# Writing out the order of four engines by hand in a fused RWKV-5 and multiplicative-FFN kernel

## The chip, the cores and the metric

One core of one Trainium2 chip. The metric is the device time of one execution in microseconds (us). Engines are called by their names in the profile: PE is the TensorE (matrix products), ACT the ScalarE, DVE the VectorE, SP the SyncE, which in these profiles only issues transfers. PSUM is the memory that TensorE's products go to here; another engine reads a bank of it out before the next product goes into it (in the changed kernel TensorE waits 9.5 us in all, three times, for a copy that does this).

## The reference, cut to what matters

```python
# attention: B, H, S, D = 4, 8, 768, 48; float32
for t in range(S):
    y[:, :, t] = r_t @ (state + (u * k_t) outer v_t)
    state = w * state + k_t outer v_t
# feed-forward on 3072 tokens of width 384; its weights come as float64
x = y.transpose(0, 2, 1, 3).reshape(3072, 384)
out = ((x @ w1) * (x @ w2)) @ w3 @ w_out      # w1, w2: 384 x 1024; w3: 1024 x 1024; w_out: 1024 x 384
```

## The kernel before

The sequence is cut into six chunks of 128 steps; a chunk of one batch row is a "unit" (24 in all). A unit costs TensorE about 2.6 us; after four units a chunk has 512 tokens, and the feed-forward takes them in eight "pairs" (x·w1 and x·w2 for 128 columns, 5.15 us a pair). w3 and w_out are multiplied with each other once ("folding"), so that the output of a chunk is then a product with one 1024 x 384 matrix, done as seven products of halves with sums of halves (Strassen-Winograd). The weights arrive as float64 and are turned into float32 by integer work shared between ScalarE and VectorE:

```python
def convert(piece, raw):                                   # 8 pieces of w1/w2, 8 of w_out, 16 of w3
    ...
    nc.scalar.activation(out=power, in_=hi.bitcast(F32), func=ABS)
    nc.vector.tensor_scalar_max(power, power, 2.0 ** -15)
    nc.vector.tensor_scalar(tb, hi, 0x80000000, None, ALU.bitwise_and)
    nc.vector.scalar_tensor_tensor(hb, pb, 3, tb, ALU.logical_shift_left, ALU.bitwise_xor)
    nc.scalar.activation(out=t, in_=lo, func=IDENTITY, bias=two, scale=2.0 ** -51)
    nc.vector.tensor_add(hb, hb, tb)
```

A load lands in one of three raw buffers. The diagonal of a unit (the u term) is three operations on VectorE and eight on ScalarE. A visit of a unit begins with the diagonal of the next one, then does half of the feed-forward steps planned beside it, then the unit's output and the next unit's products, then the other half:

```python
def diagonal(n):
    nc.vector.tensor_mul(ruk, kr[:, 0], kr[:, 1])
    nc.vector.tensor_mul(ruk, ruk, ub)
    nc.vector.tensor_reduce(dg, ruk, AX.X, ALU.add)
    for p in range(NP):
        for i in range(2):
            nc.scalar.activation(out=AT[n][:, i, p, :], in_=same, func=COPY, scale=dg[:, h:h + 1])
...
for b in range(B):                       # one visit
    scale(n + 1); diagonal(n + 1)        # or turn_rows(n + 1): ScalarE's copy of kT
    scale(n + 2); turn_blocks(n + 2)     # VectorE
    for step in plan[2 * b]: step()
    output(n)
    pairs(n + 1)
    for step in plan[2 * b + 1]: step()
```

The products of the feed-forward and of the output take turns in two PSUM banks (pool psF). What frees the first output product is a copy on ScalarE; the others are freed by additions on VectorE:

```python
def o(c, m):
    def product(a, b):
        ps = psF.tile([P, DH], F32, tag="f", ...)            # two banks
        ...
    nc.scalar.copy(out=m1, in_=product("a11", "b11"))
    nc.vector.tensor_add(top[:, :DH], product("a12", "b21"), m1)
    nc.vector.tensor_add(u2, product("s2", "t2"), m1)
    ...
```

In this kernel the order of the source is only a wish: a scheduler decides which instruction comes next on each engine.

Of the kernel before, what the change touches and what calls it, by code (L numbers as in the profile page):

```python
# [8 lines left out]
F32 = mybir.dt.float32  # L9
# [7 lines left out]
IDENTITY = mybir.ActivationFunctionType.Identity  # L17
PSUM = bass.MemoryType.PSUM


@with_exitstack
def kernel(
# [86 lines left out]
    two = const.tile([P, 1], F32)  # L109
    nc.vector.memset(two, 2.0)  # L110
# [18 lines left out]
    def load(n, which="krv"):  # L129
# [4 lines left out]
        for nm, src, dst in (("k", k, krin[n % NIN][:, 0]), ("r", r, krin[n % NIN][:, 1]), ("v", v, vnat[n % NV][:, :, :D])):  # L134
            if nm in which:
# [7 lines left out]
    ab_pieces = [(dst[:, z], src.rearrange("(q p) n -> p q n", p=P)[:, :, z * STRIP:(z + 1) * STRIP])  # L143
                 for z in range(DF // STRIP) for dst, src in ((w1, moe_w1), (w2, moe_w2))]
    sent = [0]

    def fetch(piece):

        dst, src = piece
        if src.dtype != U64:  # L150
            nc.sync.dma_start(out=dst, in_=src)
            return None
        _, m, n = src.shape
        raw = raws[sent[0] % NRAW][:, :m * n].rearrange("p (m n) -> p m n", m=m)
        sent[0] += 1
        nc.sync.dma_start(out=raw, in_=src)
        return raw
# [7 lines left out]
    landed = {0: fetch(ab_pieces[0])}  # L165
# [4 lines left out]
    landed[1] = fetch(ab_pieces[1])  # L170
# [47 lines left out]
    def body(arm, fast):  # L218
# [35 lines left out]
        def convert(piece, raw):  # L254
            dst, src = piece
            if src.dtype != U64:
                return
            _, m, n = src.shape
            lo, hi = (raw.bitcast(U32).rearrange("p m (n z) -> p m n z", z=2)[:, :, :, z] for z in range(2))
            t, power = (once.tile([P, RAW], F32, tag="cv", bufs=3 if fast else 2, name=nm)[:, :m * n].rearrange("p (m n) -> p m n", m=m)  # L260
                        for nm in ("t", "power"))
            tb, hb, pb = t.bitcast(U32), dst.bitcast(U32), power.bitcast(U32)



            nc.scalar.activation(out=power, in_=hi.bitcast(F32), func=ABS)  # L266
            nc.vector.tensor_scalar_max(power, power, 2.0 ** -15)  # L267
            nc.vector.tensor_scalar(tb, hi, 0x80000000, None, ALU.bitwise_and)
            nc.vector.scalar_tensor_tensor(hb, pb, 3, tb, ALU.logical_shift_left, ALU.bitwise_xor)  # L269

            nc.scalar.activation(out=t, in_=lo, func=IDENTITY, bias=two, scale=2.0 ** -51)  # L271
            nc.vector.tensor_add(hb, hb, tb)

        def weight(piece):
            convert(piece, fetch(piece))


        wo, w3n = {}, {}

        def out_weight(c):  # L280
            wo[c] = once.tile([P, DM], F32, tag="wo", bufs=KF, name=f"wo{c}")
            weight((wo[c][:, None, :], moe_w_out[c * P:(c + 1) * P, None, :]))

        def w3_weight(j, z):
            if z == 0:
                w3n[j] = once.tile([P, DF], F32, tag="w3", bufs=3, name=f"w3n{j}")
            js = slice(z * PIECE, (z + 1) * PIECE)
            weight((w3n[j][:, None, js], moe_w3[j * P:(j + 1) * P, None, js]))

        def fold(j):  # L290
            w3T = once.tile([P, KF, P], F32, tag="w3", bufs=3, name=f"w3T{j}")
            for i in range(2):
                ps = psF.tile([P, KF // 2, P], F32, tag="f", name=f"ps_w3T{j}_{i}")
                for q in range(KF // 2):
                    kc = i * (KF // 2) + q
                    nc.tensor.transpose(ps[:, q, :], w3n[j][:, kc * P:(kc + 1) * P], ident)
                nc.scalar.copy(out=w3T[:, i * (KF // 2):(i + 1) * (KF // 2), :], in_=ps)  # L297
            ps = psF.tile([P, DM], F32, tag="f", name=f"ps_w34_{j}")
            for kc in range(KF):
                nc.tensor.matmul(ps, lhsT=w3T[:, kc, :], rhs=wo[kc], start=(kc == 0), stop=(kc == KF - 1))  # L300
            nc.scalar.copy(out=w34[:, j, :], in_=ps)
# [12 lines left out]
        def diagonal(n):  # L314

            kr = krin[n % NIN]
            ruk = work.tile([C, H, D], F32, tag="ruk", bufs=1, name=f"ruk{n}")
            dg = work.tile([C, H], F32, tag="dg", bufs=2, name=f"dg{n}")
            nc.vector.tensor_mul(ruk, kr[:, 0], kr[:, 1])
            nc.vector.tensor_mul(ruk, ruk, ub)  # L320
            nc.vector.tensor_reduce(dg, ruk, AX.X, ALU.add)
            AT[n] = work.tile([C, 2, NP, T], F32, tag="AT", bufs=2, name=f"AT{n}")
            for p in range(NP):
                for i in range(2):
                    h = 2 * p + i
                    nc.scalar.activation(out=AT[n][:, i, p, :], in_=same, func=COPY, scale=dg[:, h:h + 1])  # L326
# [3 lines left out]
        def turned(n):  # L330
            kT[n] = work.tile([P, NP, C], F32, tag="kT", bufs=1, name=f"kT{n}")
            if fast:
                rT[n] = tts[n % 2][:, :, NP:].rearrange("x z p t -> x p z t")
            else:
                rT[n] = tts[n % 2].rearrange("x z e t -> x (z e t)").rearrange("x (e t) -> x e t", t=C)[:, NP:]

        def turn(n):
            turned(n)
            for g, dst, nm in ((0, kT, "kT"), (1, rT, "rT")):
                ps = psT.tile([P, NP, C], F32, tag="t", name=f"ps_{nm}{n}")  # L340
                for p in range(NP):
                    nc.tensor.transpose(ps[:, p, :], krs[n % NS][:, g, 2 * p:2 * p + 2, :].rearrange("t h d -> t (h d)"),
                                        ident)
                nc.scalar.copy(out=dst[n], in_=ps.rearrange("x p (z t) -> x p z t", t=Q) if fast and g else ps)
# [3 lines left out]
        scratch = {}  # L348

        def turn_blocks(n):  # L350
            tr = work.tile([P, 3, 2 * NP, Q], F32, tag="tr", bufs=1, name=f"tr{n}")
            nc.vector.transpose(out=tr.rearrange("x m e t -> x e m t"), in_=krs[n % NS][:, :, :, :D])  # L352
            scratch[n] = dram.tile([C // Q, Q, 3, Q * 2 * NP], F32, tag="scratch", bufs=2, name=f"scratch{n}")
            nc.sync.dma_start(out=scratch[n].rearrange("z f m e -> (z f) (m e)"), in_=tr.rearrange("x m e t -> x (m e t)"))
# [14 lines left out]

        def pairs(n):  # L370

            c, b = units[n]
            kk = krs[n % NS][:, 0]
            if fast:
                au = psA.tile([C, 2, 512], F32, tag="a", name=f"ps_a{n}")
                ps = au[:, :, :NP * T].rearrange("s i (p t) -> s i p t", p=NP)
            else:
                for l in range(LEVELS):
                    level(n, l)
                kk = work.tile([C, H, PAD], F32, tag="rl", bufs=1, name=f"kk{n}")  # L380
                nc.gpsimd.tensor_mul(kk, krs[n % NS][:, 0], pn[:, 0])
                au = psA.tile([C, 2, 512], F32, tag="a", name=f"ps_u{n}")

            up = au[:, :, NP * T:NP * (T + D)].rearrange("x a (p e) -> x a p e", p=NP)
            last = c == NCH - 1
            for p in range(NP):
                for i in range(2):
                    for a in range(1 if last else 2):
                        nc.tensor.matmul(up[rows(i), a, p, :], lhsT=kk[rows(a), 2 * p + i, :],  # L389
                                         rhs=vnat[n % NV][rows(a), 2 * p + i, 0:D], start=True, stop=True)  # L390
            if fast:
                for p in range(NP):
                    for a in range(2):
                        for i in range(2):
                            nc.tensor.matmul(ps[rows(a), i, p, :], lhsT=kT[n][rows(i), p, rows(a)],  # L395
                                             rhs=rT[n][rows(i), p, 2 * a:2 * a + 2], start=True, stop=True)
            by = wc.to_broadcast([P, NP, D])
            if c:
                spread(0, n)
            for a in range(1 if last else 2):  # L400
                if not c and not a:
                    if fast:
                        nc.vector.tensor_mul(st[b], up[:, a], by)
                    else:
                        nc.vector.tensor_copy(out=st[b], in_=up[:, a])
                elif fast:

                    nc.vector.tensor_add(st[b], up[:, a], st[b])
                    nc.vector.tensor_mul(st[b], st[b], by)
                else:  # L410
                    nc.vector.tensor_mul(st[b], st[b], by)
                    nc.vector.tensor_add(st[b], up[:, a], st[b])
                if not a:
                    spread(1, n)
            if fast:
# [262 lines left out]
```

## Time and profile before

| | before |
|---|---|
| median time, 4 executions | 526.04 us (525.05 to 526.63) |
| span of the profiled execution | 522.9 us |
| end of the first chunk's last pair ("the start") | 100.3 us |
| first output product begins | 232.8 us |
| from there to TensorE's last product ("the late part") | 285.9 us |

The last three rows are read from TensorE's records: the end of the 120th product of the pairs, the begin of the first 192-column product, the end of the last. 2860 TensorE products precede the first output product and 2332 are from it on. Each mark is read from one profiled execution.

### The profile page before, as it was taken

What the parts mean: (1) busy time and instruction counts of PE and PEld (TensorE: products, weight loads), DVE (VectorE), ACT (ScalarE), POOL (GpSimd) and SP (SyncE); (2) the same over time, 40 slices, a digit from 0 to 9 for tenths busy, and PEclk for the clock granted to TensorE, in tenths of its full rate; (3) what the DMA queues carried; (4) which work ended last, traced back from release to release, by engine and by line L of the source; (5) the groups of instructions that cost most, each with busy time, mean ns of one, the idle gap of its engine ahead of it and who ended that gap; (6) DMA issues with size and microseconds to landing.
All of it is one profiled execution on the core that took longest, in us unless ns stands there. A gap on an engine that the chain in (4) does not pass through costs nothing.

```text
span 522.9 us, 12272 instructions
## 1 busy us (share of the span) xinstructions
PE 495.6 (95%) x5192; PEld 324.3 (62%) x5192; DVE 281.8 (54%) x616; ACT 195.7 (37%) x487; POOL 6.0 (1%) x23
## 2 busy tenths in 40 slices
PE   2697999999999999999999999999999999999996
PEld 2586455455555656649646965498555777954486
DVE  5899897579766567492733374234432216211441
ACT  3897485566655667330223124222243110001000
POOL 4000000000000000000000000000000000000000
PEclk9887999999999999999999999999999999999999
DMA  8998565758684464230131324011120000000001
GB/s 207 230 239 236 151 149 143 197 176 207 156 253 120 164 185 117 48 91 31 57 81 45 93 77 107 32 58 50 42 77 21 1 32 31 32 30 1 0 7 60
DMA packets 96866, 52.73 MB, mean 101 GB/s; under 512 B 77729, under 2 KB 88226, under 8 KB 96802
## 3 DMA queue, kind: packets, MB, share of 16 engines
q1 hardware_dynamic: 96802, 51.86, 36.5%
q8 instruction: 43, 0.70, 0.6%
q14 instruction: 21, 0.17, 0.1%
HBM read 39.65 MB, written 12.19 MB: 99 GB/s over the span
## 4 chain that ended last, share of the span: by engine, by line
PE 85%; DVE 6%; ACT 4%; SPq 2%; issue 2%; DMA 1%; DVEq 0%; ACTq 0%
PE ps_b L505 22%; PE ps_a L500 22%; PE ps_w L300 8%; PE ps_y L483 4%; PE ps_y L473 3%; PE ps_s3t L539 3%; PE ps_s4b L539 3%; PE ps_s1t L539 3%; PE ps_a22t L539 3%; PE ps_a12b L539 3%; PE ps_s2t L539 3%; PE ps_a11b L539 3%; PE ps_a L395 2%; PE ps_a L389 1%; ACT AT L326 1%
## 5 line engine op out<-in xcount | busy, mean ns | idle before, releaser
L500 PE MATMUL ps_a<-xT,w 128*128 128x512 f32 (+1 forms) x300 | 134.8, 586 | 0.0
L505 PE MATMUL ps_b<-xT,w 128*128 128x512 f32 (+1 forms) x300 | 133.2, 578 | 0.2 <-DVE abt L506 0.2
L505 PEld LDWEIGHTS ps_b<-xT,w 128*128 128x128 f32 x300 | 56.2, 190 | 66.1 <-issue 59.6
L506 DVE TENSOR_TENSOR abt<-ps_b,a 128x512 f32<-128x512 f32 (+1 forms) x50 | 33.4, 669 | 116.6 <-PE ps_b L505 116.6
L500 PEld LDWEIGHTS ps_a<-xT,w 128*128 128x128 f32 x300 | 56.1, 192 | 58.4 <-issue 53.0
L502 ACT COPY a<-ps_a 128x512 f32<-128x512 f32 (+1 forms) x50 | 28.4, 569 | 148.4 <-PE ps_a L500 138.0
L326 ACT ACTIVATE AT<-same,dg 128x64 f32<-128x64 f32 x192 | 48.7, 336 | 0.3
L420 ACT COPY wide<-st 64x192 f32<-64x192 f32 x88 | 30.7, 348 | 43.2 <-PE ps_y L473 27.1
L300 PE MATMUL ps_w<-wo,w3T 128*128 128x384 f32 x128 | 43.1, 490 | 2.3 <-ACT w3T L297 2.3
L300 PEld LDWEIGHTS ps_w<-wo,w3T 128*128 128x128 f32 x128 | 23.7, 190 | 17.8 <-ACT w3T L297 2.8
L473 PEld LDWEIGHTS ps_y<-tt,wide 128*32 128x32 f32 x1056 | 18.4, 112 | 23.7 <-issue 15.9
L310 DVE TENSOR_TENSOR krs<-krin,pn_in 128x768 f32<-128x768 f32 x24 | 22.9, 956 | 18.1 <-PE ps_a L389 9.6
L473 PE MATMUL ps_y<-tt,wide 128*32 128x64 f32 x1056 | 25.3, 226 | 6.3 <-ACT wide L420 3.6
L271 ACT ACTIVATE t<-raw,two 128x512 f32<-128x512 uint32 (+2 forms) x32 | 25.4, 801 | 10.9 <-DVE wo L269 5.7
L266 ACT ACTIVATE power<-raw 128x512 f32<-128x512 f32 (+2 forms) x32 | 22.4, 706 | 10.6 <-DMA raw<-in_moe_w_dram 9.7
L483 PE MATMUL ps_y<-AT,vnat 64*64 64x64 f32 x1152 | 24.2, 232 | 1.6 <-DVE AT L416 1.6
L483 PEld LDWEIGHTS ps_y<-AT,vnat 64*64 64x64 f32 x1152 | 20.7, 144 | 6.4 <-DVE AT L416 2.0
L545 ACT COPY m<-ps_a11b 128x192 f32<-128x192 f32 x12 | 3.8, 319 | 53.5 <-PE ps_a11b L539 53.5
L267 DVE TENSOR_SCALAR power<-power 128x512 f32<-128x512 f32 (+2 forms) x32 | 14.0, 439 | 10.8 <-ACT power L266 10.6
L488 ACT COPY xT<-ps_y 128x384 f32<-128x384 f32 x24 | 11.4, 475 | 21.4 <-PE ps_y L483 15.8
L395 PE MATMUL ps_a<-tt,kT 64*64 64x64 f32 x768 | 18.3, 230 | 0.7 <-issue 0.7
L352 DVE STREAM_TRANSPOSE tr<-krs 128x768 f32<-128x768 f32 x19 | 18.6, 977 | 0.5
(92 smaller groups left out, 582.0 us busy)
## 6 DMA issues: line engine op xcount, KB each, us to landing
raw<-in_moe_w_dram SPq DMA_DIRECT2D x16, 512.0 KB, 4.7
scratch<-tr SPq DMA_DIRECT2D x19, 384.0 KB, 3.1
raw<-in_moe_w_dram SPq DMA_DIRECT2D x8, 768.0 KB, 5.5
tt<-scratch SPq DMA_DIRECT2D x38, 128.0 KB, 2.7
krin<-in_k_dram SPq DMA_DIRECT2D x24, 192.0 KB, 4.0
krin<-in_r_dram SPq DMA_DIRECT2D x24, 192.0 KB, 4.3
vnat<-in_v_dram SPq DMA_DIRECT2D x24, 192.0 KB, 3.6
out_dram<-osb SPq DMA_DIRECT2D x24, 192.0 KB, 1.9
```

What stands on the lines that cost most here:

```text
L271: nc.scalar.activation(out=t, in_=lo, func=IDENTITY, bias=two, scale=2.0 ** -51)
L300: nc.tensor.matmul(ps, lhsT=w3T[:, kc, :], rhs=wo[kc], start=(kc == 0), stop=(kc == KF - 1))
L326: nc.scalar.activation(out=AT[n][:, i, p, :], in_=same, func=COPY, scale=dg[:, h:h + 1])
L395: nc.tensor.matmul(ps[rows(a), i, p, :], lhsT=kT[n][rows(i), p, rows(a)], rhs=rT[n][rows(i), p, 2 * a:2 * a + 2], start=True, stop=True)
L420: nc.scalar.copy(out=wide[a][n % 2][rows(i), :, i * D:(i + 1) * D], in_=st[units[n][1]][rows(i)])
L473: nc.tensor.matmul(to(a, q, g), lhsT=wide[a][n % 2][:, p, j * Q:(j + 1) * Q], rhs=rw[:, p, 2 * a:2 * a + 2] if fast else rw[:, p, rows(a)] ...
L483: nc.tensor.matmul(ps[rows(g), a, q, :], lhsT=vv[rows(a), x:x + PAD], rhs=AT[n][rows(a), h % 2, h // 2, :], start=(a not in held and (a, g ...
L500: nc.tensor.matmul(pa[:, :n], lhsT=w1[:, z, q, js], rhs=xT[c][:, q, ts], start=(q == 0), stop=(q == KM - 1))
L502: nc.scalar.copy(out=a[:, :n], in_=pa[:, :n])
L505: nc.tensor.matmul(pb[:, :n], lhsT=w2[:, z, q, js], rhs=xT[c][:, q, ts], start=(q == 0), stop=(q == KM - 1))
L506: nc.vector.tensor_mul(abt[c, j][:, ts], pb[:, :n], a[:, :n])
L539: nc.tensor.matmul(ps, lhsT=made[c, j][a][:, m * C:(m + 1) * C], rhs=made[b][:, j, :], start=(j == 0), stop=(j == KH - 1))
```

## The change

The intent: in the start TensorE has holes since VectorE is full and works on the wrong things first, so the order of four engines is written down by hand, and for certainty the rest of the first path is placed in written order too. Conversions lose one operation; w3 is transposed one block ahead of its use; its loads are issued by ScalarE; four of the first diagonals are placed by VectorE.

```diff
+START = """
+d.0 N.0 e.0 M.0 k.0 f.0 T.0 H.0 g.0 U.0 R.0 d.1 i.0 k.1 p.0 e.1 r.0 kr.2 ...
+ ... (one word per step, 271 words, to the last pair of the first chunk)
+U.8 l.8 u.0.6.2 S.7 i.8 p.8 V.7 j.8 A.8 z.9 Y.7 a.0.7.2 m.8 b.0.7.2 c.0.7.2 u.0.7.2
+"""
 ... conversion
-            nc.scalar.activation(out=power, in_=hi.bitcast(F32), func=ABS)
-            nc.vector.tensor_scalar_max(power, power, 2.0 ** -15)
+            nc.scalar.activation(out=dst, in_=words(i)[1].bitcast(F32), func=ABS, scale=2.0 ** -112)
-            nc.scalar.activation(out=t, in_=lo, func=IDENTITY, bias=two, scale=2.0 ** -51)
+            nc.scalar.activation(out=part["t", i], in_=words(i)[0], func=COPY, scale=2.0 ** -29)
 ... w_out and w3: five operations of a piece spread over three steps, loads from ScalarE
+        def convert_on(i):
+            for step, x in ((total, i - 2), (magnitude, i), (high, i - 1), (sign, i), (low, i - 1)):
+                if NAB <= x < len(pieces):
+                    step(x)
+            if NAB < i:
+                fetch(i - 1 + NRAW, nc.scalar)
 ... the plan behind the start
+        def late(rest, folds, cut):
+            visits(2, merge(rest, folds[:cut]))
+            visits(3, ... + [sums_of_weights] + SUMS(0)[:2] + AB(2, range(1, 2)) + SUMS(0)[2:] + ... + O(0) + ...)
+            visits(4, O(1) + merge(SUMS(2), AB(3, range(3))) + O(2) + AB(3, range(3, KF)))
+            visits(5, merge(SUMS(3), AB(4, range(3))) + O(3) + AB(4, range(3, KF)))
+            for step in merge(SUMS(4), AB(5, range(3))) + O(4)[:1] + AB(5, range(3, KF)) + SUMS(5) + O(4)[1:] + O(5):
+                step()
+            with tc.manual_schedule(engines={PE, ACT, DVE, SP}):
+                for name, *at in (word.split(".") for word in START.split()):
+                    names[name](*map(int, at))
+                for i in range(NAB, NAB + NRAW):
+                    fetch(i, nc.scalar)
+                late(AB(1, ...), FOLD(convert_on, 2), 25)
```

(The letter of a word is a step, the number its unit or piece: d, e and f are VectorE's three operations of a diagonal, M, N, H, L and Q the five operations of a conversion, a and b the products of a pair, c and u ScalarE's copy and VectorE's multiplication behind them. Cut: the helpers that split a unit into steps, the second set of buffers for the sums, the general path for other values of w, which this input does not take.)

## The prediction

> **What bounds the kernel now.** I read the page's busy shares first, then the slices, the waits of the TensorE, narrow windows, the timeline. Shares and slices (a digit is tenths of a slice of 13.1 us, a fortieth of 522.9):
>
> ```profile
> PE 495.6 (95%) x5192; PEld 324.3 (62%) x5192; DVE 281.8 (54%) x616; ACT 195.7 (37%) x487; POOL 6.0 (1%) x23
> ...
> PE   2697999999999999999999999999999999999996
> ...
> DVE  5899897579766567492733374234432216211441
> ACT  3897485566655667330223124222243110001000
> ...
> PEclk9887999999999999999999999999999999999999
> ```
>
> TensorE is the bound; the only slices under 9 are the first four and the last. VectorE (DVE) is fullest exactly there, and the granted clock is lower there. So there is something to win only in the first 55 us or so, and a little later. How much, the waits of the TensorE tell:
>
> ```profile
> PE ps_p L208 <- DVE both L205: 7.6, 1, 7.6
> PE ps_y L473 <- ACT wide L420: 3.6, 3, 2.1
> PE ps_y L473 <- issue: 2.4, 2, 2.0
> PE ps_w L300 <- ACT w3T L297: 2.3, 3, 1.0
> PE ps_kT L342 <- DVE krs L310: 1.8, 1, 1.8
> PE ps_y L483 <- DVE AT L416: 1.6, 2, 1.3
> PE ps_kT L342 <- ACT kT L344: 1.3, 1, 1.3
> ```
>
> Without the first row (the preamble, which stays) and the small rows this is 13.0 us, of which L300 (2.3 us) is the folding of w3 into w_out. Windows (us, busy per engine with instructions, clock, DMA share, GB/s):
>
> ```profile
> 20.00:40.00 20.00, 17.66 (x446) 14.88 (x438) 19.54 (x39) 19.10 (x53) 0.00 (x0) 0.85 0.94 246
> 40.00:60.00 20.00, 16.48 (x192) 11.79 (x192) 19.16 (x36) 12.73 (x28) 0.00 (x0) 0.83 0.79 218
> ...
> 280.00:300.00 20.00, 19.65 (x280) 18.02 (x279) 8.82 (x21) 5.75 (x18) 0.00 (x0) 1.00 0.33 90
> 300.00:320.00 20.00, 20.00 (x191) 11.83 (x190) 13.32 (x33) 5.57 (x15) 0.00 (x0) 1.00 0.35 91
> ```
>
> From 20 to 60 us VectorE has no idle time; what matters is which work it does first. From 300 to 500 us TensorE never stops: there the scheduler's order leaves nothing to win, and a new order can only lose.
>
> [...] TensorE is busy only 1.49 of the 5 us from 40 us on, and from 45 to 50 us the clock is 0.50; six 256-column matmuls take 2.77 us there against 1.46 elsewhere. Window by window of 5 us from 15 to 50 us, busy time times the missing clock share is 0.2 + 1.0 + 1.3 + 0.3 + 2.5, about 5 us lost. [...] Here an issue takes some 0.4 us and landing 4.4 us (below)[...]. [...] the trace has 691 ns for the 128x512 multiplication. I take 0.69 us for the new diagonal.
>
> **The change part by part.** Durations, from the groups by line and the issues:
>
> ```profile
> L326 ACT ACTIVATE AT<-same,dg 128x64 f32<-128x64 f32 x192 | 48.7, 336 | 0.3
> ...
> L267 DVE TENSOR_SCALAR power<-power 128x512 f32<-128x512 f32 (+2 forms) x32 | 14.0, 439 | 10.8 <-ACT power L266 10.6
> ...
> raw<-in_moe_w_out_dram SPq DMA_DIRECT2D x8, 384.0 KB, 4.4
> ```
>
> *Shorter conversion.* Removes the 32 maximum operations, 14.0 us of VectorE, 8 of them (556 ns each, 4.4 us) in the first 60 us. *Diagonals on VectorE for units 1, 3, 5, 7.* ScalarE loses 4 x 8 activations (eight take 2.0 us in the timeline, so 8 us), VectorE gains 4 x 0.69 = 2.8 us. Neither engine is the bound beyond the start, so both matter only there.
>
> *Written order of the start (to the end of the first chunk's eight w1/w2 pairs).* In the timeline of before this work ends at 100.2 us, having begun at 11.4. TensorE's own work in it: 8 pairs x 5.15 + 9 units x 2.5 + 5 turned units x 1.2 = 70 us. Of the 89 us, 9.3 are idle and about 5 lost to the clock. Going down the written list with the durations of before, VectorE's list is 69 us long, so it is over at 80 us at the earliest and still sets the pace to about 65 us; after that TensorE does, and I get 87 us with no hand-over costs. I take 89: **gain 11 us** (7 to 13).
>
> *Folding, in strict order.* Now every instruction of the first path, not only the start, stays in written order, and the w_out/w3 conversions begin only after the start is over (the scheduler had put the first two w_out loads at 55 and 60 us). 13 conversion steps precede the first turn of w3, which stands after four pairs and two units: 4 x 5.15 + 2 x 2.6 = 26 us of TensorE work. Three raw buffers allow a load for every step only when the step two before has given its buffer up, so two steps take a landing (4.4) plus a step on ScalarE (0.55 + 0.65 + 0.4 for issuing): 3.0 us a step. Ten steps so bound take 30 us, after some 7 us for the first three: 37 against 26 us. ScalarE waits in order, so its copies of ps_a wait too, and TensorE behind them on its two PSUM buffers: about 11 us lost where before lost 2.9, **-8 us**. For the rest of the folding the one-block lead removes the waits on w3T and some breaks in the order: **+2 us**.
>
> *Last three chunks, in strict order.* Where a visit begins with an output product right after a pair, ScalarE does eight diagonals and the kT copy before the copy that frees the first product's PSUM buffer. From the pair's end: multiplication 0.7, ruk and dots 1.4 more, diagonals 2.0, kT 0.6, copy 0.3 = 5.1 us; two products keep TensorE for 2.6. Lost 2.5 us; this stands at the first output product of chunks 1, 2 and 3, for chunk 3 with a sums step (1.7 us) ahead: 2.5 + 2.5 + 4.2. At the end, the last sums (16 x 0.42 = 6.7 us) stand on VectorE right after the last pair and before the reader of the second of the following products: 0.7 + 6.7 + 0.4 = 7.8 us against three products of 1.3: 3.9 lost. Before, the scheduler spread these; TensorE idles nowhere there. Sum 13.1, less about 1 us of small waits that go: **-12 us**.
>
> Sum: +11 - 8 + 2 - 12 = -7, so about 534 us.
>
> **Rivals.** (a) *The start alone counts, later order is as good as the scheduler's.* For: the changed plan puts output work and a second set of sums buffers exactly where strict order would stop VectorE, so whoever wrote it thought of it; lead and extra buffers are for this. Against: the queue positions above. Then +11 to +15: 512 to 516 us. (b) *Loads take over the start.* The DMA share is 0.9 up to 40 us, so earlier order cannot bring weights earlier than bytes arrive (eight w1/w2 strips of 768 KB, nine units, three transposes: some 13 MB at 215 to 245 GB/s, 55 to 60 us). For: weight pairs 6 and 7 need the last of them at about 60. Against: pairs before them give 25 us of work. It would take 3 to 5 us of the gain: 537. (c) *Idle time halves the clock*: [...] 1 to 3 us more; but fewer holes at 40 us also spare the low clock there (in my 11).
>
> **Range and chances.** My sum says 534; each of its four terms is uncertain by 3 to 5 us, together some 8. Rival (a) has a weight of about a third, as my latencies may be too long by a microsecond a step: that draws the point to 528 us. The 80% range is 515 to 540. Faster by over 2% (under 516.3) needs nearly no new stops: 0.15. Slower by over 2% (over 537.1) needs only my stops plus a start a little worse: 0.22. Within 2%: 0.63.
>
> **What would show it.** Start: the first chunk's last pair ends at about 89 us instead of 100.2, with VectorE at 19 of 20 us from 20 to 60. Folding: ScalarE's magnitude operations wait for raw by DMA for well over the 10 us of before, and TensorE waits for copies of ps_a and conversion totals, some 11 us between 90 and 130 us. Late: waits of TensorE for the copy m three times by 2.5 to 4 us, and for osb or u near the end by about 4. If the chunk-1 pairs follow each other without gaps, the folding step fails; if the slices after 250 us are all 9 with no such waits, the late step fails, and the time is that of rival (a). A start that still ends after 96 us makes the first term wrong.

## More of the kernel before

Every time quoted is a median of four or more executions.

The views that carry the argument are shown in the prediction. One more line is used later. It is the stretch from 120 to 140 us, in which before does its first folding work; columns are the stretch, its length, busy us (and instructions) of PE, weight loads, DVE, ACT and POOL, then the granted clock, the share of the transfer engines and GB/s:

```profile
120.00:140.00 20.00, 18.72 (x301) 10.71 (x294) 17.69 (x36) 15.40 (x40) 0.00 (x0) 1.00 0.72 177
```

TensorE is busy 18.7 of 20 us at full clock here, beside a nearly full VectorE.

## The result, and the profile after

The changed kernel takes **551.2 us** (549.07 to 551.98, four executions) against 526.04: slower by 4.7%, ratio 1.0474 with an interval of 1.0436 to 1.0512. (Ratios here are the mean time of one kernel's runs over that of the other's of the same rounds, so not quite the ratio of the medians.) It lies outside the predicted range.

| us | before | after | difference |
|---|---|---|---|
| the start ends | 100.3 | 91.5 | -8.8 |
| fifth pair of the second chunk begins | 126.8 | 133.7 | +6.9, so 15.7 lost since |
| first output product begins | 232.8 | 236.7 | +3.9, so 3.0 regained |
| late part | 285.9 | 308.7 | +22.8 |

At the second mark after has done one transposition of w3 (1.1 us) more than before, so the front of the folding, the stretch from the first mark to the second, lost 14.6 us and the rest, up to the third, regained 1.9.

The page of after, busy shares and slices:

```profile
PE 500.8 (91%) x5192; PEld 329.0 (60%) x5192; DVE 279.2 (51%) x587; ACT 183.0 (33%) x455; POOL 6.0 (1%) x23
...
PE   2899999695999999999989998999888999999796
...
PEclk9999999986999999999999998999898999999999
```

The first slices are 8 and 9 now, as intended. Below 9 are slices 8 and 10 (96 to 110 and 124 to 138 us, the front) and single slices from 275 us on, where before had none but the last. TensorE's busy time rose by 5 us for the same 5192 products, while the clock line (PEclk, the granted clock in tenths) has 8s and a 6 in or beside the same slices: products ran at half clock for a part of them. VectorE and ScalarE are not fuller than before.

The waits of the TensorE, after (line waited for, then us in all, how often, the longest):

```profile
PE ps_s2t L659 <- ACT m L665: 9.5, 3, 4.1
PE ps_w3T L326 <- DVE w3n L303: 6.6, 2, 4.1
PE ps_a L604 <- ACT a L610: 5.2, 2, 4.8
PE ps_s3t L659 <- DVE osb L666: 3.1, 1, 3.1
PE ps_a L464 <- ACT kT L430: 2.9, 1, 2.9
```

(A row of the preamble, unchanged, and those under 2.9 us are cut.) The first, fourth and fifth are the stalls of the late part; the second and third, but for 0.4 us, are those of the front: 11.4 us, where TensorE had no idle time at all in before. (m is the copy that empties an output product's first bank, osb the output rows on their way to memory, a the copy of a pair's product, kT a unit's turned k.) The windows that answer to those of before (start, then front):

```profile
20.00:40.00 20.00, 18.87 (x507) 15.96 (x507) 17.55 (x32) 14.55 (x35) 0.00 (x0) 1.00 0.80 193
40.00:60.00 20.00, 20.00 (x273) 12.28 (x272) 19.90 (x37) 12.53 (x27) 0.00 (x0) 1.00 0.83 226
...
120.00:140.00 20.00, 13.43 (x30) 6.25 (x31) 13.49 (x26) 11.71 (x27) 0.00 (x0) 0.74 0.74 199
```

From 20 to 60 us TensorE went from 34.1 to 38.9 us busy and from a clock of 0.84 to 1.00: that is the gain. For the same 1417 products of the start TensorE was idle 5.0 us less (18.7 to 13.7) and busy 3.8 us less (81.6 to 77.8, the clock's part): together the 8.8. (The clock column also says 1.00 where no record exists: up to 22.2 us the products of after were still slow, 64x64 ones took 316 ns against 222 later.) From 120 to 140 us it is busy 13.4 us instead of 18.7, at a clock of 0.74.

One late stall in full, from the timeline of after around the first output product (start, duration, instruction; in brackets the idle time before it and what ended it), first TensorE:

```profile
285.08 1.46 PE L659 MATMUL ps_a12b<-w,abt 128*128 128x192 f32 x8
289.21 1.57 PE L659 MATMUL ps_s2t<-t,raw 128*128 128x192 f32 x8 [2.67 <-ACT m L665]
```

and ScalarE in the same time:

```profile
286.42 2.02 ACT L369 ACTIVATE AT<-same,dg 128x64 f32<-128x64 f32 x8 [4.43 <-DVE dg L358]
288.35 0.60 ACT L430 COPY kT<-tt 128x512 f32<-128x512 f32 x1
288.85 0.30 ACT L665 COPY m<-ps_a11b 128x192 f32<-128x192 f32 x1
```

The copy m, which frees the first product's bank, needs 0.30 us and has its input at 285.2 us. In written order it stands behind eight diagonals that wait for VectorE's dots, and behind the copy of kT. ScalarE is idle for 4.43 us just before: a short instruction that is ready waits behind one that is not. Here that costs the copy 3.6 us, from 285.2 to 288.85 us.

### The profile page after: what moved, and what is told of

It is laid out like the page before. It is cut to its first block, busy times and chain, and to the rows that moved or that the text cites. A ratio compares the mean times of both kernels' runs of the same rounds, so it can differ in the third digit from the quotient of the medians.

```text
span 550.2 us, 12210 instructions
## 1 busy us (share of the span) xinstructions
PE 500.8 (91%) x5192; PEld 329.0 (60%) x5192; DVE 279.2 (51%) x587; ACT 183.0 (33%) x455; POOL 6.0 (1%) x23
## 4 chain that ended last, share of the span: by engine, by line
PE 81%; DVE 6%; ACT 6%; DMA 3%; issue 2%; ACTq 0%; SPq 0%; DVEq 0%
PE ps_a L604 21%; PE ps_b L604 20%; PE ps_w L332 8%; PE ps_y L578 4%; PE ps_s2t L659 3%; PE ps_s3t L659 3%; PE ps_a22t L659 3%; PE ps_s4b L659 3%; PE ps_y L564 3%; PE ps_s1t L659 3%; PE ps_a L464 3%; ACT AT L369 2%; DMA raw<-in_moe_w_dram 2%; PE ps_a L457 2%; PE ps_a11b L659 2%
## 5 line engine op out<-in xcount | busy, mean ns | idle before, releaser
L604 PE MATMUL ps_a<-xT,w 128*128 128x512 f32 (+1 forms) x300 | 139.3, 602 | 5.2 <-ACT a L610 5.2
L369 ACT ACTIVATE AT<-same,dg 128x64 f32<-128x64 f32 x160 | 40.4, 335 | 55.4 <-DVE dg L358 50.4
L480 DVE TENSOR_TENSOR st<-ps_a,st 128x192 f32<-128x192 f32 x40 | 14.2, 355 | 29.2 <-ACT wide L489 24.4
L300 ACT ACTIVATE t<-raw 128x512 uint32<-128x512 uint32 (+2 forms) x32 | 22.5, 703 | 15.9 <-DVE w3n L296 9.9
L564 PEld LDWEIGHTS ps_y<-tt,wide 128*32 128x32 f32 x1056 | 16.2, 111 | 12.8 <-issue 10.1
L342 DVE TENSOR_TENSOR krs<-krin,pn_in 128x768 f32<-128x768 f32 x24 | 22.8, 948 | 0.0
L659 PE MATMUL ps_s3t<-w,abt 128*128 128x192 f32 x96 | 19.2, 346 | 3.1 <-DVE osb L666 3.1
L564 PE MATMUL ps_y<-tt,wide 128*32 128x64 f32 x1056 | 20.3, 223 | 1.0 <-ACT tt L401 1.0
L464 PEld LDWEIGHTS ps_a<-tt,kT 64*64 64x64 f32 x768 | 15.8, 141 | 7.2 <-ACT kT L430 3.8
## 6 DMA issues: line engine op xcount, KB each, us to landing
tt<-scratch SPq DMA_DIRECT2D x38, 128.0 KB, 2.9
```

Source lines behind the costliest of these rows:

```text
L300: nc.scalar.activation(out=part["t", i], in_=words(i)[0], func=COPY, scale=2.0 ** -29)
L342: nc.vector.tensor_mul(krs[n % NS][:, :, :, :D], kr, pn[:, :, :, :D])
L464: nc.tensor.matmul(upper(n)[rows(a), i, p, :], lhsT=kT[n][rows(i), p, rows(a)], rhs=rT[n][rows(i), p, 2 * a:2 * a + 2], start=True, stop=True)
L564: nc.tensor.matmul(yt[n][g * Q:(g + 1) * Q, a, q, :], lhsT=wide[a][n % 2][:, p, j * Q:(j + 1) * Q], rhs=rw[:, p, 2 * a:2 * a + 2] if fast ...
L604: nc.tensor.matmul(ps, lhsT=(w1 if x == "a" else w2)[:, z, q, js], rhs=xT[c][:, q, ts], start=(q == 0), stop=(q == KM - 1))
L659: nc.tensor.matmul(ps, lhsT=made[c, j][a][:, m * C:(m + 1) * C], rhs=made[b][:, j, :], start=(j == 0), stop=(j == KH - 1))
```

## The experiments

The marks of all sixteen runs; the time before was 526.1 to 526.6 us in their rounds.

| run | time us | ratio | start ends | first output product | late part |
|---|---|---|---|---|---|
| before | 526.0 | | 100.3 | 232.8 | 285.9 |
| after | 551.2 | 1.047 | 91.5 | 236.7 | 308.7 |
| e_start_only | 528.9 | 1.002 | 110.8 | 237.2 | 285.4 |
| e_start_fold | 527.3 | 1.001 | 91.6 | 235.0 | 285.9 |
| e_four_banks | 538.3 | 1.022 | 93.0 | 237.3 | 293.3 |
| e_heads_tail | 540.0 | 1.027 | 91.9 | 239.3 | 293.9 |
| e_early_wout | 544.6 | 1.035 | 96.9 | 230.1 | 307.7 |
| e_low_free | 548.5 | 1.042 | 93.0 | 233.0 | 309.8 |
| e_half_slots | 553.6 | 1.050 | 93.3 | 238.4 | 309.0 |
| e_dots_first | 551.4 | 1.047 | 92.8 | 236.6 | 308.7 |
| e_front_all | 543.3 | 1.032 | 93.4 | 227.9 | 312.1 |
| e_front_sync | 541.9 | 1.030 | 92.9 | 226.4 | 310.4 |
| e_early_low | 537.3 | 1.021 | 95.1 | 220.9 | 308.4 |
| e_sync_queue | 550.1 | 1.044 | 91.9 | 235.5 | 308.8 |
| e_before_conv | 527.4 | 1.003 | 102.0 | 234.7 | 286.2 |
| e_best | 516.0 | 0.982 | 96.5 | 224.2 | 285.7 |
| e_best_later | 515.9 | 0.979 | 96.6 | 224.5 | 286.2 |
| e_best_dots | 516.0 | 0.981 | 96.5 | 223.6 | 285.3 |

Five of these kernels have the very same start (after, e_start_fold, e_four_banks, e_half_slots, e_sync_queue), and it ends between 91.5 and 93.3 us: a difference of under 2 us between two marks shows nothing.

### Which part of the written order costs

**e_start_fold**: written order up to the end of the visits that hold most of the folding, the scheduler from there on.

```diff
-                late(AB(1, ...), FOLD(convert_on, 2), 25)
+                folds = FOLD(convert_on, 2)
+                visits(2, merge(AB(1, ...), folds[:25]))
+            rest_of(folds, 25)           # outside the block: visits(3), (4), (5) and the tail, same plan
```

> The changed kernel in written order for the start and for the visits of chunk 2, which hold the folding of w3 into w_out; the scheduler orders what follows. Theory: the folding's front stays as slow as in the changed kernel (chunk 1's pair 4 begins near 133.7 us, about 14.5 us lost against before), while the stalls of the late part go with what they cost in half clock: from the first output product to the end 286 to 289 us instead of 308.7, so 551.2 - 21 = 530 us (527 to 533). With the run that frees all but the start this splits the loss in two. Rival (the late stalls come from the plan and not from the order): 545 to 551 us.

Measured 527.3 us, as the theory had it. The late part is 285.9 us, that of before to the tenth; with the same plan, the same buffers and the same banks as after. TensorE's slices have the holes of the front and none behind them:

```profile
PE   2899999966989999999999999999999999999996
```

The whole 22.8 us of the late part come from the written order, none from the plan.

**e_start_only**: only the start in written order.

```diff
-                for i in range(NAB, NAB + NRAW): fetch(i, nc.scalar)
-                late(...)
+            for i in range(NAB, NAB + NRAW): fetch(i, nc.scalar)      # outside the block
+            late(...)
```

> The changed kernel with only its start (to the last w1/w2 pair of the first chunk) in written order; everything after it goes back to the scheduler, with the same plan, the same loads from ScalarE's queue, the same one-block lead of w3 and the same two PSUM banks for output products. Theory (the written order behind the start is what costs): the start keeps its gain (its last pair ends near 91.3 us as in the changed kernel, 100.1 before), the waits for the copy m at the first output products of chunks 1 to 3 (2.7, 2.7, 4.1 us) and for osb at the end (3.1 us) are gone, and the time is 526.0 - 8.8 = 517 us, 1 to 2 less for the w3 lead: 514 to 519. Rival (the new plan behind the start, its load queue or its bank use costs, in whatever order): above 535 us, with the m waits still there.

Measured 528.9 us. Half of the theory fell. The late part is 285.4 us, but the start ends at 110.8 us, later than before. The order on ScalarE tells why: with the following work free to move, the scheduler put all eight conversions of w_out ahead of the last copy of the start; the first stands at 57.4 us. So a block in written order protects itself only as far as what follows it is held back too. And it shows that the start's gain and the conversions of w_out compete for the same engines: before does two of the eight conversions and most of a third before its start ends, after none (the first is at 96.4 us).

### The late part

**e_four_banks**: nothing moves on any engine, but output products have four banks.

```diff
+                made["turn"] = 1 - made.get("turn", 1)
+                pool, tag = ((psT, "t"), (psF, "f"))[made["turn"]]
-                ps = psF.tile([P, DH], F32, tag="f", ...)
+                ps = pool.tile([P, DH], F32, tag=tag, ...)
```

> Written order everywhere, as changed; the output products after the folding take turns over four PSUM banks instead of two (the two banks of the transposes are idle by then). Nothing moves on any engine. Theory (two banks make TensorE wait for a copy that stands late on ScalarE or VectorE): two more products, 2.6 us, may go ahead, so the waits of 2.7, 2.7 and 4.1 us for m go to 0, 0 and about 1.5 us, that of 3.1 us at the end to about 1; 10 us less. And as each of these stalls is followed by a window at half clock that costs TensorE 1 to 2 us, and those go too, 4 to 6 us more: 535 to 538 us. Rival 1 (half-clock windows do not depend on the stalls): 541 us. Rival 2 (the engines behind are late on the whole, so the wait moves to the next product): 547 to 551 us.

Measured 538.3 us, between the theory's 538 and rival 1's 541. The timeline of TensorE at the first output product of this run:

```profile
285.61 1.46 PE L661 MATMUL ps_a12b<-w,abt 128*128 128x192 f32 x8
286.91 1.46 PE L661 MATMUL ps_s2t<-t,raw 128*128 128x192 f32 x8
```

The 2.67 us are gone: TensorE goes on while ScalarE is as late as before. The late part fell by 15.4 us; 9.5 of m and 3.1 of osb were waits, 3.6 of other waits came in their place (1.6 for a sum, 1.5 for m, 0.5 for osb), so some 6 of the 15.4 (an estimate, by difference) are clock. In its records the half-clock windows (stretches of 3.4 us at half clock, see below) at 333, 387, 415 and 520 us, which after has, are all absent. The one at 387 us is no work of the four banks, though: the 2.9 us for kT ahead of it are still there, but they fall across two windows and leave TensorE busy about 1.7 us of the emptier one, where in after it was 0.50.

**e_heads_tail**: two moves in the written order instead.

```diff
-            for step in (rk, rku, dots, place): step(n)
+            for step in (rk, rku, dots): step(n)
+            place(n, nc.vector if fast else None)
-  ... AB(5, range(3, KF)) + SUMS(5) + O(4)[1:] + O(5)
+  ... AB(5, range(3, 7)) + SUMS(5)[:3] + AB(5, range(7, KF)) + O(4)[1:] + SUMS(5)[3:] + O(5)
```

> The changed kernel with two edits in its written order. All later diagonals are placed by VectorE (one operation of 0.69 us) instead of by eight of ScalarE (2.0 us); and of the last sums three of four steps stand before the last pair and the fourth after the first of the following products. Theory (the m waits come from ScalarE's queue at a visit's head, that for osb from the sums): the m waits of 2.7, 2.7 and 4.1 us become waits for VectorE's addition, which stands some 5.1 us after the pair's end against three products of 1.3: 1.2, 1.2 and 2.9 us; osb at the end 3.1 to 0; two of the four half-clock windows go (2 to 3 us); ScalarE's 2 us per visit in the folding's front give 2 more: 538 to 543 us. Rival (the stalls have another cause than the order on these two engines): 547 to 552 us.

Measured 540.0 us. The waits for m are gone; 2.9 us for osb (three times, none over 1.4) and 2.3 for a sum stand in their place. Late part 293.9 us, with one half-clock window left (at 336 us). Its front gained nothing (first output product at 239.3 us), so ScalarE's 2 us per diagonal, taken away alone, are not what holds the front.

**The clock.** In the trace of after the granted clock falls to 0.50 at 107.5, 128.0, 332.8, 387.4, 414.7 and 520.5 us: all are multiples of 3.413 us apart (6, 66, 82, 90, 121 from the first). It stays there for 3.41 us in the last four and for 6.83 and 10.24 us, two and three times as long, in the first two. A window is here one step of this grid. Four of them, after:

```profile
284.98:288.39 3.41, 1.56 (x10) 1.26 (x8) 3.18 (x5) 1.97 (x9) 0.00 (x0) 1.00 0.00 0
288.39:291.80 3.41, 2.59 (x16) 2.59 (x17) 0.71 (x2) 0.77 (x3) 0.00 (x0) 1.00 0.29 115
329.40:332.81 3.41, 0.76 (x5) 0.46 (x3) 3.31 (x7) 2.74 (x10) 0.00 (x0) 1.00 0.02 7
332.81:336.22 3.41, 3.39 (x11) 3.39 (x12) 1.14 (x4) 0.00 (x0) 0.00 (x0) 0.50 0.28 108
```

A stall of 2.67 us falls across two windows in the first case, TensorE is busy 1.56 of 3.41 us in the emptier one, and the clock stays. In the second, as long, it falls into one window, busy 0.76 us, and the next window runs at half clock. With all 18 traces laid on their grids, this is more than one pair: each of the 62 full-clock windows in which TensorE was busy under 1.43 us was followed by half clock, none of the 2524 with over 1.67 us was, and of the ten between, four were (in before and after alone: ten of ten, none of 277, one of two). So what counted in these traces is some 2 us of idle time (3.41 less 1.43) within one window, and the same stall of 2.67 us came with half clock or without. Four half-clock windows in the late part cost about 4 x 3.4 x 0.5 = 6.8 us (an estimate from their length and the clock of 0.50). Three of them follow a predicted stall and one (at 387 us) the wait of 2.95 us for kT. With 12.6 us of predicted stalls and the 2.95 for kT this makes 22.3 of the 22.8 us.

### The front of the folding

**e_half_slots** tests the mechanism that the prediction gave for it.

```diff
+            if NAB <= i < NAB + KF:                      # w_out: six half buffers
+                slot = raws[(i - NAB) // 2 % NRAW][:, i % 2 * RAW // 2:]
-                for i in range(NAB, NAB + NRAW): fetch(i, nc.scalar)
+                for i in range(NAB, NAB + 2 * NRAW): fetch(i, nc.scalar)
```

> The changed kernel; the eight loads of w_out use half of a raw buffer each, so six are on their way at once instead of three (w3 keeps three whole ones). Theory of the prediction (the load round trip with three buffers sets 3.0 us a step in the folding's front): the eight w_out steps no longer wait for loads, 8 to 10 us less, 541 to 543 us. Rival (ScalarE and VectorE wait for each other and for other work in their written order; loads are mostly hidden behind that): 0 to 3 us less, 548 to 551 us.

Measured 553.6 us, not faster than after, where 541 to 543 would have shown the mechanism: it does not set the pace. ScalarE's waits from 90 to 140 us, after and then this run:

```profile
ACT w3n L288 <- DMA raw<-in_moe_w_dram: 4.4, 3, 2.2
ACT t L300 <- DVE wo L296: 3.3, 4, 1.2
```

```profile
ACT t L306 <- DVE wo L302: 5.6, 6, 1.2
ACT t L306 <- DVE w3n L302: 2.0, 3, 1.2
ACT w3n L294 <- DMA raw<-in_moe_w_dram: 1.1, 2, 0.7
```

Waits for loads of w3 fell from 4.4 to 1.1 us (for w_out they were only 0.4 us in after, by the line's own view), and the waits for VectorE inside the conversions rose from 4.6 (3.3 and 1.3 for w3n) to 7.6. One took the place of the other. The edit has a cost of its own, too. ScalarE's queue at the head of the front:

```profile
90.75 6.14 ACTq L175 DMA_DIRECT2D raw<-in_moe_w_out_dram  x6
```

Six issues in a row hold it for 6.14 us, where the three of after take 1.34 (why is not shown), and its next operation begins 3.7 us behind the start's end instead of 2.5. So 1.2 us were lost by the test itself, not the 8 to 10 that were to be won.

**e_low_free**: ScalarE's low words get a buffer of their own, so that they do not wait for VectorE's high words of the same piece.

```diff
+        room = once.tile([P, 2 * RAW], U32, ...)          # three slots of 512 words instead of two of 768
+            part["t", i] = slot(i, 1)
             nc.scalar.activation(out=part["t", i], in_=words(i)[0], func=COPY, scale=2.0 ** -29)
```

> The changed kernel, but in each conversion ScalarE's low words go to a buffer of their own (three buffers of 512 words in the room of the two of 768), so that the operation on the low words no longer waits for VectorE's operation on the high words of the same piece, only for one of a piece earlier. Theory (the folding's front is slow because ScalarE and VectorE wait for each other in turn within each conversion, and the copies of ps_a stand behind such a wait in ScalarE's order): 5 to 8 us less, 543 to 546 us. Rival (the load round trip with three raw buffers alone sets the pace there): 549 to 552 us.

Measured 548.5 us, between the theory's 543 to 546 and the rival's 549: 3.7 us less at the first output product.

**e_early_wout**: the eight conversions of w_out written into the last third of the start.

```diff
-p.5 Q.6 j.5 ... x.8 p.6 a.0.6.2 ... b.0.7.2 c.0.7.2 u.0.7.2
+p.5 Q.6 W.8 W.9 W.10 j.5 ... m.6 w.8 b.0.5.2 ... x.8 p.6 w.9 a.0.6.2 ... w.14 b.0.7.2 c.0.7.2 w.15 u.0.7.2
-            for i in range(NAB, len(pieces) + lag + 1):
+            for i in range(NAB + KF, len(pieces) + lag + 1):
```

> Written order everywhere, as changed, but the eight conversions of w_out (loads and all five operations each) are written into the last third of the start, between its last three w1/w2 pairs, where ScalarE and VectorE have idle time; the folding then begins with w3. Theory (the folding's front is slow because 13 conversion steps with a load round trip each stand before its first turn): with 8 of them out of the way the front loses 2 to 4 us instead of 14.5, its two half-clock windows (at 107 and 128 us) go, the start stays within 1.5 us: 551.2 - 11 to 13 = 538 to 540 us. Rival (ScalarE's and VectorE's in-order exchange of other work, diagonals, states, copies, is the slow part): 4 to 5 us less, 546 to 547 us.

Measured 544.6 us: 6.6 us less at the first output product, though the start ends 5.4 us later. The expected 11 to 13 us were too high; the rival's 4 to 5 is nearer.

**e_early_low**: both together.

> Both of the above together, all in written order: w_out converted in the last third of the start, and a buffer of its own for the low words. The run with w_out early gave 544.6 us and lost 9 us between the work of 40 and of 100 us. Theory (those 9 us are the exchange between ScalarE and VectorE inside the conversions): 538 to 540 us, the wait for a at 113 us (3.2 us) gone. Rival (they are the waits for diagonals and states): 543 to 545 us.

Measured 537.3 us. The first output product begins at 220.9 us, 15.8 us earlier than after; singly the two gave 3.7 and 6.6. TensorE's waits for the copy a fell from 3.6 us with w_out early alone to 1.0.

**e_dots_first, e_front_all, e_front_sync**: is it three waits in series? At the head of the front ScalarE waits 4.4 us for the dots of unit 9, which stand on VectorE behind the start's last multiplication (the waits view puts this down to a load, since that came last by its records; the timeline shows dg).

```diff
-... m.8 b.0.7.2 c.0.7.2 u.0.7.2
+... m.8 d.9 e.9 f.9 g.9 b.0.7.2 c.0.7.2 u.0.7.2           (e_dots_first)
 + low words' own buffer + half buffers                     (e_front_all)
 + fetch(..., nc.sync) instead of nc.scalar                 (e_front_sync)
```

> The changed kernel with the diagonal of unit 9 (three operations on VectorE, eight on ScalarE) written ahead of the start's last b product instead of behind its multiplication. Theory (ScalarE stands idle 4.4 us there, and the first conversion with it; the front is a chain that begins with this wait): 3 to 6 us less, 545 to 548 us. Rival (other waits cover it, as they did with the loads): 549 to 552 us.

> The changed kernel with the three edits of the front together: diagonal of unit 9 early, low words in their own buffer, half buffers for the loads of w_out. Theory (three waits in series, each covered by the next if it is removed alone; alone they gave what the run before this list shows, 2.7 us and nothing): at 100 us of TensorE work at most 3 us behind before instead of 7.5, its half-clock windows mostly gone, 538 to 543 us. Rival (the work on ScalarE and VectorE between 91 and 134 us, some 26 and 32 us busy of 42, with hand-overs, is too much for that stretch wherever the waits stand): 546 to 549 us.

> The same three edits and the loads issued from SyncE instead of ScalarE. Theory (ten issues of 0.33 us and as many waits of 0.4 us for its own last operation stand in ScalarE's order in that stretch): 2 to 4 us less than the run with the three edits. Rival (they lie in time in which ScalarE waits anyway): within 1 us of it.

Measured 551.4, 543.3 and 541.9 us. At the first output product, against after: dots first -0.1, low words -3.7, half buffers +1.7; the three together -8.8 us. Counted from the start's own end, which leaves its variation out, it is -1.4, -5.2 and -0.1, together -10.7. Either way the three give 4 us or more beyond their sum: the waits are in series and cover each other. How much of that is the waits alone is not shown, since half-clock windows go as well (in the front after has five, the three single runs three, four and four, the joint one has one). In e_front_sync the issues no longer hold ScalarE at the head (its copy of kT begins at 92.4 us, in e_front_all at 97.2), but its further 1.5 us are inside the variation of single runs (after's four differ by 2.9 us) and are left open. The late part of e_front_all is 312.1 us, 3.4 more than after, since in its records two half-clock windows follow the first late stall (at 280 us), which in after has none behind it. Its profiled execution, at 546.7 us the slowest of four, is therefore only 5.3 us faster than that of after; the medians differ by 7.9.

**e_sync_queue**: loads from SyncE again.

```diff
-                fetch(i - 1 + NRAW, nc.scalar)
+                fetch(i - 1 + NRAW, nc.sync)
```

> The changed kernel with the loads of w_out and w3 issued from SyncE's queue again, at the same places of the written order. Theory: ScalarE gets rid of some 27 issues of 0.33 us and of as many waits of 0.4 us for its own last operation before them, while a load stands behind SyncE's other waits: nearly even, 548 to 553 us. Rival 1 (SyncE's order holds loads back, which is what the ScalarE queue was for): over 555 us. Rival 2 (the issues in ScalarE's order are a cause of the slow front): under 546 us.

Measured 550.1 us: the queue makes no difference that this run could show. (The expectation counted too much for ScalarE: in its timeline in after the gap at an issue is 0.41 us in all, 0.33 of it the issue.) The loads of w_out took 3.6 us to land in after, issued by ScalarE, and 4.4 in before, issued by SyncE (medians; why they differ is not shown).

**e_before_conv**: the shorter conversion alone, in the kernel before.

```diff
-            nc.scalar.activation(out=power, in_=hi.bitcast(F32), func=ABS)
-            nc.vector.tensor_scalar_max(power, power, 2.0 ** -15)
+            nc.scalar.activation(out=power, in_=hi.bitcast(F32), func=ABS, scale=2.0 ** -112)
-            nc.scalar.activation(out=t, in_=lo, func=IDENTITY, bias=two, scale=2.0 ** -51)
+            nc.scalar.activation(out=tb, in_=lo, func=COPY, scale=2.0 ** -29)
```

> The kernel before with the shorter conversion alone (scale 2^-112 in ScalarE's absolute value, no maximum on VectorE, low words by a plain scaled copy). Theory (14 us of VectorE go, 4.4 of them in the first 60 us, where VectorE is full and sets the pace): 2 to 4 us less, 522 to 524 us. Rival 1 (the scheduler fills the room with other work and the order of the start is what counts): within 1 us of before. Rival 2 (the shorter conversion is the larger part of the start's 9 us): under 520 us.

Measured 527.4 us, ratio 1.003 (0.999 to 1.007): nothing, although VectorE is busy 12 us less (281.8 to 269.6). The theory fell. Shorter work on the fullest engine does not pay by itself while the order stays with the scheduler. So the start's gain needs the order; whether the order alone would do, and what the early diagonals give, was not tried.

### Both lessons put together

**e_best**: start and folding in written order, w_out converted early, low words in their own buffer, the last three chunks left to the scheduler.

```diff
 e_early_low
-                late(AB(1, ...), FOLD(convert_on, 2), 17)
+                folds = FOLD(convert_on, 2)
+                visits(2, merge(AB(1, ...), folds[:17]))
+            rest_of(folds, 17)
```

> Start and folding in written order with w_out converted early and the low words' own buffer; the last three chunks left to the scheduler. Theory (gain of the start kept by feeding the conversions early, no stalls late): at the first output product 4 us ahead of before from w_out early alone, 8 to 9 with the buffer, and nothing lost after it: 516 to 522 us, the fastest so far. Rival (a faster front only makes the scheduler's later part wait more, or its gain is given back): 524 to 528 us.

Measured 516.0 us (514.5 to 520.6), ratio 0.982 (0.976 to 0.988): faster than both kernels, by about 2% than the one before (so the verdict at a threshold of 2% is "unclear"; that it is faster is not, since the interval excludes 1). From its page, TensorE's slices:

```profile
PE   2999997999999999999999999999999999999996
```

One slice is below 9 between the first and the last, at 80 us; the late part is at before's 285.7 us. Of the 8.6 us gained by the first output product 8.1 are there at the end (span 514.8 against 522.9).

**e_best_later** and **e_best_dots** tried to close the hole at 80 us: the first moves two early conversions behind the copies of kT and a, the second has the diagonal of unit 9 early, as above.

```diff
-x.8 p.6 w.9 a.0.6.2 l.7 j.6 y.8 u.0.5.2 w.10 A.7 c.0.6.2 U.7
+x.8 p.6 a.0.6.2 l.7 j.6 y.8 u.0.5.2 w.9 A.7 c.0.6.2 w.10 U.7          (e_best_later)
-... m.8 w.14 b.0.7.2
+... m.8 d.9 e.9 f.9 g.9 w.14 b.0.7.2                                     (e_best_dots)
```

> The fastest version so far (start and folding written out, w_out early, own buffer for the low words, the rest left to the scheduler: 516.0 us) with the second and third early conversion moved behind the copy of kT and the copy of a that they stood ahead of on ScalarE. Theory (TensorE's wait of 1.7 us for kT at 76 us and the half-clock window at 83 us that follows come from these): 3 us less, 512 to 514 us. Rival (the conversions are then late at the first turn of w3, and the wait moves there): 516 to 519 us.

> The fastest version (516.0 us) with the diagonal of unit 9 ahead of the start's last b product. Theory (the wait at the head of the folding also holds this version): 2 to 4 us less, 512 to 514 us. Rival (with w_out converted before, nothing waits behind it): 515 to 517 us.

Measured 515.9 and 516.0 us, ratios 0.979 (0.976 to 0.981) and 0.981 (0.979 to 0.983): no gain over e_best from either. In e_best_dots the rival was right. In e_best_later the wait for kT fell from 1.7 to 0.5 us, and one of 1.1 us for xT, at a unit's products, came in its place; it did not move to the first turn of w3, as the rival had it. All three end their start at 96.5 us and reach the first output product within a microsecond of each other.

## Why the prediction was wrong

**The bound and the start: right in the main.** TensorE is the bound, and the written order gained in the start; that VectorE's order alone had held it was not shown apart from the other edits. Predicted gain 11 (7 to 13), measured 8.8; from 20 to 60 us TensorE's holes went as foreseen, with VectorE at 17.6 and 19.9 of 20 us instead of 19. The new diagonal took 688 ns on VectorE, against the 0.69 us that were taken. The shorter conversion, to which the prediction gave a part of it, gave nothing alone.

**The folding's front: the cause was wrong, and the sum left out a term (8 predicted, 14.6 measured).** The step that failed is "two steps take a landing (4.4) plus a step on ScalarE": e_half_slots gave the loads their room and nothing was won, and ScalarE's magnitude operations wait 4.8 us for loads there, not "well over the 10 us of before". In its place stand three waits in series, two of them between ScalarE and VectorE, in strict order. That the pace came out all the same is luck: the first twelve magnitude operations begin from 96.4 to 131.4 us, 3.2 us a step against the predicted 3.0, and TensorE waits 11.4 us, against the predicted 11, for what was named (4.8 for the copy a, 6.6 for totals of w3). Two things then made 8 out of 11 and 14.6 out of 11.4. The prediction took off 2.9 us that before was to lose in the same stretch, but before has no idle time of TensorE in it. And it left out the clock: 3.2 us up to the fifth pair and 5.5 in the whole folding (an estimate: half of TensorE's busy time) in the five half-clock windows at 107.5 and 128 us, in which products took up to twice their time (six of 512 columns 5.25 us from 109.5 us on, against 2.74 to 2.84 at full clock).

**The rest of the folding: the size was right** (+2 predicted, +1.9 measured). The waits on w3T (2.3 us) went as foreseen, but 2.4 us of others came (1.6 for a, 0.8 "issue") and 2.3 us of half clock, so where the 1.9 us come from is not shown.

**The late part: the mechanism was right, the term mis-sized (12 predicted, 22.8 measured).** The stalls that the prediction worked out stand in the trace as 2.67, 2.67, 4.13 and 3.08 us, 12.6 against 13.1 in sum, at the places named; e_start_fold, e_four_banks and e_heads_tail each remove them by another way. Missing from the sum were 2.95 us for kT at 387 us, where a visit has no steps between a pair and the unit, and 6.8 us of half clock, behind three of these stalls and the wait for kT. Rival (c) had the clock, but only for the folding and at "1 to 3 us more"; in the late part a stall of 2.67 us was enough.

**From sum to range.** The sum of the steps was 534 us; the point was drawn to 528 by rival (a), which had a weight of a third and no measurement behind it. e_start_fold shows what rival (a) was worth: with the same plan in written order the late part loses 22.8 us, with the scheduler's order none. Terms that all err in one direction, since a missed wait can only cost, had been given a symmetric range.

What stays open: what the single waits marked "issue" at unit products between 80 and 91 us are (1.8 us in e_best), and which share of the start's gain belongs to the diagonals on VectorE.

## What to carry to other kernels

Write out an order only for the stretch where the profile shows that the scheduler's order loses, hold back what follows it, and leave the rest to the scheduler: here the written order gained 8.8 us in the start and lost 22.8 us where TensorE had had no waits. When an engine that is off the bound is made to start later, its work does not vanish; look for the hole in the start into which it fits, and if removing one wait changes nothing, remove its neighbours with it before calling it harmless. To a stall of TensorE add the half-clock window that followed in these traces each time the stall left it busy for under 1.43 us of a 3.41 us window: about 1.7 us each here (an estimate, half of the window).
